# Dealing PSUM reads and gate steps over later units, accumulating DMAs in twos, and the last block's sums late from DRAM

## The chip, the cores and the metric

The kernel runs on one core of a Trainium2 chip. The metric is the device time of one execution in microseconds (us). A difference of some 0.3% (8 to 9 us here) is about what the measurement can tell from none.

## The reference, cut to what matters

```python
X = np.fft.fft(np.fft.fft(x, axis=1), axis=2).real          # x: 4 x 3072 x 256
h = X.reshape(12288, 256) @ w_in                             # 256 -> 2048
x = np.where(h > 0, h, np.exp(np.minimum(h, 0)) - 1) @ w_out # 2048 -> 256
h = np.maximum(x @ moe2_w_in, 0)                             # 256 -> 1024
u, v = h[..., :512], h[..., 512:]
v_n = (v - mean(v)) / np.sqrt(var(v) + 1e-6)                 # over the 512
v_s = einsum('ts,bsd->btd', w_spatial, v_n) + b_spatial      # 3072 x 3072, 4 batches
out = (u * v_s) @ moe2_w_out                                 # 512 -> 256
```

## The kernel before, in words

All matrix products are made in float32 as three products of rounded parts (`matmul3`, L180 to L182): a high part, which ScalarE (ACT) makes with a copy into the type fp32r, and a low part, the rest, which VectorE (DVE) makes with a subtraction. So every operand costs an ACT cast and a DVE subtraction before TensorE (PE) can use it.

The program has three stages. Up to about 170 us it makes the Fourier transform and prepares weights. From 170 to about 1290 us (the FFN stage) it works through 16 blocks of tokens, 8 groups to a block. While a block runs, the "pieces" of the block before it are made between its matmuls: six `v_piece` (one PSUM tile `pv`, ReLU on ACT at L670 into one of four buffers `v`, mean and deviation on GpSimd (POOL), the normalisation on DVE at L692) and eight `u_piece` (ACT at L717 into one of two buffers `uu`, then a DMA). The last stage does not use v itself but sums over subsets of its six token thirds: `V_SETS` lists 14 of them, and `v_d` holds one array of DRAM for each. A piece writes its v to the first array by a plain store on SyncE (SP, L735) and adds it to the others by accumulating DMAs on POOL's queue (L733), which `run_norms` issues all at once: up to five behind each other for one v. `finish` makes the pieces of the last block, while the last stage's first operands are prepared between them.

The last stage (from about 1300 us) is the product with w_spatial, by a scheme with 15 products instead of 18 (`PRODUCTS`). It is a list of 240 units (b, r, c, p): two batch pairs b, 15 products r, two column halves c, four steps p of the contraction. A unit is 24 matmuls 128x512 into the four PSUM banks `a` of its c. Its operand w is a sum of one to three blocks of w_spatial, its operand v one of the arrays above (a difference of two in one product); v is shared by the two c. Per unit the kernel writes down, in one fixed order on each engine, what I call emission k:

- if a gate is cut, `project` (24 matmuls 128x512 with w_out, names `gh`, `gl`, `wo2`) and `put` (ACT copy and store);
- `operands(k)`: `low` (DVE, L855, into `wlo` with two buffers or `vlo`) of the operands whose high part was made in emission k-1, that is those of unit k+1; `gate(k)`: one or two `multiply` (DVE, sum times u, L912) and, if a gate is being cut, four `cut_low` at once (DVE, L921, tile `gl`); `add` (DVE, L843, the sum of the loaded blocks `raw`, one instruction less than blocks) and `high` (ACT, L849) for unit k+2; and `load` (SP queue, L832, into one of 8 buffers `raw`) for unit k+4;
- the unit's 24 matmuls;
- after a unit with p = 3 its four `collect`, or eight where a product goes to two sums (DVE, L905: they read the PSUM banks into `sum`), all at once.

So DVE's order is the order of the emissions, and what is slow there delays the low parts behind it. Units 6 to 11 also load and convert w_out of the last product from a 64-bit format in four parts (`load_wo2`; names `wo2b`, `wo2r`, L146 to L166), each part using one `raw` buffer. The bounds of the emissions are not marked in the trace; the first unit starts at 1317.6 us, unit 16 at 1431.8, unit 239 at 2822.1.

Of the kernel before, what the change touches and what calls it, by code (L numbers as in the profile page):

```python
# [123 lines left out]
def fourier_ffn_gated_kernel(ctx: ExitStack, tc: tile.TileContext, t, out: bass.AP):  # L124
# [9 lines left out]
        for b in range(0, B, 2) for x in V_SETS for p in range(KP)  # L134
    }
    u_d = [[dram.tile([P, NJ, BLK], F32, name=f"u{b}{c}") for c in range(4)] for b in range(B)]

# [511 lines left out]
    def v_piece(i, k):  # L649
# [72 lines left out]
    def run_pieces(n):  # L722
        for _ in range(min(n, len(pieces))):
            kind, *a = pieces.pop(0)
            (v_piece if kind == "v" else u_piece)(*a)
        for d in deviations:
            d()
        deviations.clear()

    def run_norms(n=None):  # L730
# [15 lines left out]
    for s in range(NG + LAG):  # L746
# [76 lines left out]


    raws, highs, ready = {}, {}, {}

    def load(key):
        kind, k = key
        raws[key] = []
        for sg, src in (v_terms if kind == "v" else w_terms)(k):  # L830
            raw = rp.tile([P, 2, TC], F32, tag="raw", bufs=RAWS, name="raw")
            nc.sync.dma_start(raw, src)  # L832
            raws[key].append((sg, raw))

    def operand_tile(kind, x):
        if kind == "v":
            return th.tile([P, 2, HV], F32R, tag=f"v{x}", name=f"v{x}")
        return wq.tile([P, 2, TC], F32R, tag=f"w{x}", bufs=3 if x == "hi" else 2, name=f"w{x}")

    def add(*key):  # L840
        (_, x), *more = raws[key]
        for sg, y in more:
            nc.vector.tensor_tensor(x, x, y, op=ALU.add if sg > 0 else ALU.subtract)  # L843
        raws[key] = x

    def high(*key):
        x = raws.pop(key)
        hi = operand_tile(key[0], "hi")
        nc.scalar.copy(hi, x)  # L849
        highs[key] = hi, x  # L850

    def low(*key):
        hi, x = highs.pop(key)
        lo = operand_tile(key[0], "lo")
        nc.vector.tensor_tensor(lo, x, hi.bitcast(F32), op=ALU.subtract)  # L855
# [12 lines left out]

    us, biases, sums, parts, gates, gated, cutting = {}, {}, {}, {}, [], [], []

# [26 lines left out]
    def collect(b, r, c, accs, j, cols=slice(0, TC)):  # L897
# [8 lines left out]
        if j == NJ - 1:  # L906
            for n, m in completed(r):
                gates.extend(((b + n, MC * m + c), x) for x in range(NJ))

# [58 lines left out]

    def gate(k):


        for _ in range(2 if gates and gates[0][0][1] % MC == 1 or len(gates) > NJ or k >= NU - KP else 1):
            if gates:
                key, j = gates.pop(0)
                multiply(key, j)
                if j == NJ - 1:
                    gated.append((key, k))
                    del us[key]
        if cutting:
            for j in range(NJ):  # L980
                cut_low(cutting[0], j)

    def operands(k):

        for key in steps.get(k - 1, []) if k else []:
            low(*key)
        if gated and gated[0][1] < k and k + 1 < NU and idle(k + 1):
            key, _ = gated.pop(0)
            for j in range(NJ):
                cut_high(key, j)  # L990
            cutting.append(key)
        gate(k)
        for key in steps.get(k, []):
# [9 lines left out]
    for k in range(-2, 0):  # L1003
# [8 lines left out]
        finish(2)  # L1012
    finish(len(pieces) + 2)
    ffn.close()
    first.close()
# [8 lines left out]
    def bank(c, j):  # L1024
        return ps.tile([P, TC], F32, tag=f"a{c}{j}", name=f"a{c}{j}")

    accs = [None] * MC
    turn = 0
    for k, (b, r, c, p) in enumerate(units):
        if cutting:  # L1030
            key = cutting.pop()
            pos = [bank(1 - c, 2 * turn + o) for o in range(2)]
            turn = 1 - turn
            for j in range(NJ):
                project(key, pos, j)
            put(key, pos)
        operands(k)
        if WO2 <= k < WO2 + NJ:
            load_wo2(k - WO2)
# [22 lines left out]
        if p == KP - 1 and k < NU - 1:  # L1062
            for j in range(NJ):
                collect(b, r, c, accs[c], j)
    assert not gates and not gated and not cutting
    (n, m), = completed(r)
# [77 lines left out]
```

## Time and profile before

| | us |
|---|---|
| median of 3 runs | 2835.91 (2832.69 to 2841.42) |
| profiled execution | 2839.11, with a span of 2837.3 |
| PE busy | 2696.8 (95% of the span) |
| DVE busy | 2098.6 (74%) |
| ACT, POOL busy | 1308.7 (46%), 703.8 (25%) |
| mean granted TensorE clock | 0.977 |

The profiled execution took 3 us more than the median of the three runs. Its span leaves out 1.8 us around the program. All times of the trace count from the span's start. Busy matmuls are pipelined: one 128x512 matmul is shown as 0.39 us, but they start 0.227 us apart.

### The profile page before, as it was taken

The numbers are of one execution on the slowest core, as the hardware profiler recorded it, in microseconds if no ns is written. First come the engines' busy times: TensorE is split into PE (matmuls) and PEld (weight loads), VectorE is DVE, ScalarE is ACT, GpSimd is POOL, SyncE is SP. The second block draws the span as 40 slices with busy tenths as digits, with TensorE's granted clock in tenths as the row PEclk, the third lists the DMA queues.
The fourth block names the chain that finished last, engine by engine and source line by source line (L and its number), as shares of the span: only waits on it lengthen the run. The fifth ranks groups of instructions, "written<-read, shape, count | busy, mean of one in ns | idle before, by whom it ended". The sixth has DMA issues, their size and how long they took to land.

```text
span 2837.3 us, 35269 instructions
## 1 busy us (share of the span) xinstructions
PE 2696.8 (95%) x12854; PEld 2373.8 (84%) x12854; DVE 2098.6 (74%) x2541; ACT 1308.7 (46%) x1676; POOL 703.8 (25%) x1079
## 2 busy tenths in 40 slices
PE   5867999999999999997899999999999999999999
PEld 5757999999999999996687878787787887878877
DVE  8878888888878888883657657676756676676776
ACT  3456777777767777773222232333232222232332
POOL 5367244445543544456100000000000000000000
PEclk8989999999999999998899999999999999999999
DMA  5521466666774666779868668677767677677773
GB/s 224 184 74 42 154 144 144 142 152 144 145 150 152 144 154 148 147 164 260 262 224 283 226 215 274 230 261 251 252 207 262 228 244 251 227 259 249 260 242 135
DMA packets 211728, 561.15 MB, mean 198 GB/s; under 512 B 24777, under 2 KB 49370, under 8 KB 210018
## 3 DMA queue, kind: packets, MB, share of 16 engines
q1 hardware_dynamic: 145720, 435.10, 44.7%
q0 software_dynamic: 43520, 92.29, 18.0%
q10 hardware_dynamic: 22314, 31.51, 3.1%
q8 instruction: 100, 1.64, 0.2%
q14 instruction: 74, 0.61, 0.1%
HBM read 388.90 MB, written 169.91 MB: 197 GB/s over the span
## 4 chain that ended last, share of the span: by engine, by line
PE 72%; DVE 14%; DMA 4%; POOL 3%; issue 3%; ACT 3%; SPq 0%; ACTq 0%; DVEq 0%; POOLq 0%
PE a L181 13%; PE a L182 13%; PE a L180 13%; PE acc L181 5%; PE acc L182 5%; PE acc L180 5%; DVE raw L843 4%; DVE sum L905 2%; DVE vlo L855 2%; PE pv L181 1%; PE pv L180 1%; PE pv L182 1%; PE po L180 1%; PE pu L180 1%; PE po L181 1%
## 5 line engine op out<-in xcount | busy, mean ns | idle before, releaser
L181 PE MATMUL a<-wlo,vhi 128*128 128x512 f32 x1920 | 753.3, 392 | 18.0 <-DVE wlo L855 17.9
L182 PE MATMUL a<-whi,vlo 128*128 128x512 f32 x1920 | 752.8, 392 | 4.3 <-DVE vlo L855 4.3
L180 PE MATMUL a<-whi,vhi 128*128 128x512 f32 x1920 | 751.9, 392 | 1.6 <-ACT vhi L849 1.6
L849 ACT CAST whi<-raw 128x1024 fp32r<-128x1024 f32 x240 | 252.0, 1052 | 954.9 <-DVE raw L843 673.8
L855 DVE TENSOR_TENSOR wlo<-raw,whi 128x1024 fp32r<-128x1024 f32 x240 | 293.6, 1223 | 401.7 <-PE a L181 177.8
L181 PEld LDWEIGHTS a<-wlo,vhi 128*128 128x128 f32 x1920 | 362.8, 189 | 98.3 <-DVE wlo L855 22.1
L182 PEld LDWEIGHTS a<-whi,vlo 128*128 128x128 f32 x1920 | 363.1, 189 | 82.5 <-DVE vlo L855 6.6
L180 PEld LDWEIGHTS a<-whi,vhi 128*128 128x128 f32 x1920 | 363.2, 189 | 79.8 <-ACT vhi L849 3.4
L181 PE MATMUL acc<-glo,wo1h 128*128 128x384 f32 (+1 forms) x1024 | 350.9, 343 | 22.5 <-POOL glo L606 16.2
L180 PE MATMUL acc<-ghi,wo1h 128*128 128x384 f32 (+1 forms) x1024 | 348.6, 340 | 0.0
L182 PE MATMUL acc<-ghi,wo1l 128*128 128x384 f32 (+1 forms) x1024 | 348.2, 340 | 0.0
L894 POOL DMA_DIRECT2D u<-u x32 | 24.0, 752 | 1275.2 <-DVE sum L912 1000.5
L606 DVE TENSOR_TENSOR glo<-h,ghi 128x1536 fp32r<-128x1536 f32 (+3 forms) x128 | 221.0, 1727 | 137.7 <-ACT ghi L599 137.3
L843 DVE TENSOR_TENSOR raw<-raw 128x1024 f32<-128x1024 f32 x248 | 302.8, 1223 | 3.3
L733 POOL DMA_DIRECT2D v<-v x256 | 230.5, 1270 | 75.2 <-DVE v L692 46.4
L592 DVE SCALAR_TENSOR_TENSOR h<-e,h 128x1536 f32<-128x1536 f32 (+1 forms) x128 | 231.9, 1811 | 0.0
L581 ACT ACTIVATE e<-h 128x1536 f32<-128x1536 f32 (+1 forms) x128 | 190.0, 1484 | 88.6 <-DVE h L573 81.9
L181 PEld LDWEIGHTS acc<-glo,wo1h 128*128 128x128 f32 x1024 | 195.1, 191 | 28.8 <-POOL glo L606 18.8
L599 ACT CAST ghi<-h 128x1536 fp32r<-128x1536 f32 (+1 forms) x128 | 187.7, 1467 | 20.1 <-DVE h L592 20.1
L182 PEld LDWEIGHTS acc<-ghi,wo1l 128*128 128x128 f32 x1024 | 195.4, 191 | 0.0
L180 PEld LDWEIGHTS acc<-ghi,wo1h 128*128 128x128 f32 x1024 | 194.5, 190 | 0.1
L586 ACT ACTIVATE e<-e 128x1536 f32<-128x1536 f32 (+1 forms) x128 | 190.2, 1486 | 0.0
(198 smaller groups left out, 4441.9 us busy)
## 6 DMA issues: line engine op xcount, KB each, us to landing
raw<-in_wT SPq DMA_DIRECT2D x480, 512.0 KB, 5.2
v<-v POOLq DMA_DIRECT2D x256, 256.0 KB, 6.5
raw<-v SPq DMA_DIRECT2D x128, 512.0 KB, 4.1
v<-v SPq DMA_DIRECT2D x224, 256.0 KB, 3.0
u<-uu ACTq DMA_DIRECT2D x128, 192.0 KB, 3.5
u<-u POOLq DMA_DIRECT2D x16, 1024.0 KB, 7.5
q<-in_xq SPq DMA_DIRECT2D x12, 1032.0 KB
out<-sum SPq DMA_DIRECT2D x48, 256.0 KB, 2.1
```

What stands on the lines that cost most here:

```text
L180: nc.tensor.matmul(acc, lhsT=w[0], rhs=x[0], start=start, stop=False, skip_group_check=more)
L181: nc.tensor.matmul(acc, lhsT=w[0], rhs=x[1], start=False, stop=False, skip_group_check=more)
L182: nc.tensor.matmul(acc, lhsT=w[1], rhs=x[0], start=False, stop=stop, skip_group_check=more)
L581: nc.scalar.activation(e[:, :, :w], st[s]["h"][:, :, :w], AF.Relu, scale=-1.0)
L586: nc.scalar.activation(e[:, :, :w], e[:, :, :w], AF.Exp, scale=-1.0)
L592: nc.vector.scalar_tensor_tensor(out=h[:, :, :w], in0=e[:, :, :w], scalar=-1.0, in1=h[:, :, :w], op0=ALU.add, op1=ALU.max)
L599: nc.scalar.copy(st[s]["hi"][:, :, :w], st[s]["h"][:, :, :w])
L606: eng.tensor_tensor(st[s]["lo"][:, z, :w], st[s]["h"][:, z, :w], st[s]["hi"][:, z, :w].bitcast(F32), op=ALU.subtract)
L733: nc.gpsimd.dma_start(dst, v, accum_op=ALU.add)
L843: nc.vector.tensor_tensor(x, x, y, op=ALU.add if sg > 0 else ALU.subtract)
L849: nc.scalar.copy(hi, x)
L855: nc.vector.tensor_tensor(lo, x, hi.bitcast(F32), op=ALU.subtract)
```

## The change

Four things are done.

- In the last stage `operands(k)` keeps only `low`, `add`, `high` and `load`. What was in `gate`, and the `collect` at the end of a unit, goes into a queue (`waiting`, `keys`), and `rest(k, n)` behind `operands(k)` takes n pieces of it: `spare(k)` is 8, less two for each low part and each addition of the emission, eight more in the last 16 units and after a projection. Collects must go at the latest three units later. `project` comes once all four `cut_low` of a gate are written, in a unit whose other banks are free. One projection is left for after the last unit.
- `wlo` gets a third buffer. v is loaded straight into the buffer of its low part, `vlo`, where the subtraction then works in place; `raw` has 7 buffers for 8. The steps at which v is prepared move from (-6, -2, -1, 1) to (-6, -1, 0, 1).
- In the FFN stage the accumulating DMAs go into a list, and two are issued at a time (`run_sums(2)`), twice per group.
- The v of the last block is stored once, to a new array `v_last`, by plain stores on SP. Its 30 accumulating DMAs are issued in the last stage, from DRAM to DRAM, one every second unit from unit 16 on, on POOL's queue.

```diff
@@ norm (in v_piece)
+            if last:
+                stores.append((v_last[at // 2][:, at % 2], v, False))
+                return
@@ run_pieces, run_norms
+        run_sums(2)
+    def run_sums(n):
+        for dst, v in sums_due[:n]:
+            nc.gpsimd.dma_start(dst, v, accum_op=ALU.add)
+        del sums_due[:n]
             if more:
-                nc.gpsimd.dma_start(dst, v, accum_op=ALU.add)
+                sums_due.append((dst, v))
@@ the loop over the groups, behind run_norms()
+        run_sums(2)
@@ the last stage
-    RAWS = 8
+    RAWS = 7
+    HALVES = 8
+    LATE = 16
...
-        return p - 2 if r == 0 else MC * KP * r + (-6, -2, -1, 1)[p]
+        return p - 2 if r == 0 else MC * KP * r + (-6, -1, 0, 1)[p]
...
-    def gate(k):
-        for _ in range(2 if gates and gates[0][0][1] % MC == 1 or len(gates) > NJ or k >= NU - KP else 1):
-            if gates:
-                key, j = gates.pop(0)
-                multiply(key, j)
-                if j == NJ - 1:
-                    gated.append((key, k))
-                    del us[key]
-        if cutting:
-            for j in range(NJ):
-                cut_low(cutting[0], j)
+    def spare(k):
+        n = HALVES - 2 * len(steps.get(k - 1, []))
+        for kind, i in steps.get(k, []):
+            n -= 2 * (len((v_terms if kind == "v" else w_terms)(i)) - 1)
+        return n + (HALVES if k >= NU - 4 * KP else 0)
+
+    def rest(k, n):
+        while waiting and (n > 0 or waiting[0][0] <= k):
+            collect(*waiting.pop(0)[1:])
+            n -= 1
+        for x in keys:
+            while n > 0 and x["done"] < NJ:
+                multiply(x["key"], x["done"])
+                x["done"] += 1
+                n -= 1
...
+            while n > 0 and x["low"] < NJ and x["cut"] < k:
+                cut_low(x["key"], x["low"])
+                x["low"] += 1
+                n -= 1
@@ the loop over the units
-        if cutting:
-            key = cutting.pop()
+        n = spare(k)
+        if keys and keys[0]["low"] == NJ and idle(k) and not waiting:
+            key = keys.pop(0)["key"]
...
+            n += HALVES
         operands(k)
+        rest(k, n)
...
+        if LATE <= k and k % 2 == 0 and later:
+            dst, src = later.pop(0)
+            nc.gpsimd.dma_start(dst, src, accum_op=ALU.add)
...
         if p == KP - 1 and k < NU - 1:
-            for j in range(NJ):
-                collect(b, r, c, accs[c], j)
+            waiting += [(k + KP - 1, b, r, c, accs[c], j) for j in range(NJ)]
```

DVE of the kernel before, emissions 51 to 53 (a low part of v, the additions, the four reads of the banks after unit 51, and two gates cut right behind):

```order
L855 TENSOR_TENSOR vlo<-raw,vhi 128x1024
L843 TENSOR_TENSOR raw<-raw 128x1024 x2
L905 TENSOR_TENSOR sum<-bias,a_15020 128x512
L905 TENSOR_TENSOR sum<-bias,a_15021 128x512
L905 TENSOR_TENSOR sum<-bias,a_15022 128x512
L905 TENSOR_TENSOR sum<-bias,a_15023 128x512
L855 TENSOR_TENSOR wlo<-raw,whi 128x1024
L921 TENSOR_TENSOR gl<-sum,gh 128x512 x4
L843 TENSOR_TENSOR raw<-raw 128x1024 x2
L855 TENSOR_TENSOR wlo<-raw,whi 128x1024
L921 TENSOR_TENSOR gl<-sum,gh 128x512 x4
L843 TENSOR_TENSOR raw<-raw 128x1024 x2
```

The same gates in the kernel after: the first is multiplied and cut in emissions 44 to 47 (its projection stands ahead of unit 54, for 53 before):

```order
L932 TENSOR_TENSOR sum<-sum,u 128x512 x2
L876 TENSOR_TENSOR wlo<-raw,whi 128x1024
L932 TENSOR_TENSOR sum<-sum,u 128x512 x2
L876 TENSOR_TENSOR wlo<-raw,whi 128x1024
L860 TENSOR_TENSOR raw<-raw 128x1024 x2
L941 TENSOR_TENSOR gl<-sum,gh 128x512 x2
L876 TENSOR_TENSOR wlo<-raw,whi 128x1024
L860 TENSOR_TENSOR raw<-raw 128x1024 x2
L941 TENSOR_TENSOR gl<-sum,gh 128x512 x2
L876 TENSOR_TENSOR wlo<-raw,whi 128x1024
```

and the reads after unit 51 stand in emissions 52 and 53, in twos behind the additions, with the second gate's steps behind them (its projection is ahead of unit 57, for 54 before):

```order
L876 TENSOR_TENSOR wlo<-raw,whi 128x1024
L860 TENSOR_TENSOR raw<-raw 128x1024 x2
L926 TENSOR_TENSOR sum<-bias,a_14987 128x512
L926 TENSOR_TENSOR sum<-bias,a_14988 128x512
L876 TENSOR_TENSOR wlo<-raw,whi 128x1024
L860 TENSOR_TENSOR raw<-raw 128x1024 x2
L926 TENSOR_TENSOR sum<-bias,a_14989 128x512
L926 TENSOR_TENSOR sum<-bias,a_14990 128x512
L876 TENSOR_TENSOR wlo<-raw,whi 128x1024
L932 TENSOR_TENSOR sum<-sum,u 128x512 x4
L876 TENSOR_TENSOR wlo<-raw,whi 128x1024
L941 TENSOR_TENSOR gl<-sum,gh 128x512 x4
```

What moved: no low part of an operand stands behind four or eight reads and four cuts in a row any more.

POOL of the kernel before, in the last block's pieces (`v_...` are arrays of sums in DRAM, `v` the buffer in SBUF):

```order
L688 TENSOR_SCALAR w<-w 128x1
L689 TENSOR_TENSOR y<-y,w 128x1
L733 DMA v_1245_1_164<-v 128x512
L733 DMA v_245_1_172<-v 128x512
L733 DMA v_25_1_176<-v 128x512
L733 DMA v_35_1_184<-v 128x512
L733 DMA v_45_1_192<-v 128x512
L684 TENSOR_SCALAR ve<-sums 128x1
```

and POOL of the kernel after, behind the conversion of w_out in the last stage (`vl_...` is the new array):

```order
L166 TENSOR_TENSOR wo2r<-wo2r,wo2b_13783 128x256
L1082 DMA v_1245_1_164<-vl_195 128x512 x2
L1082 DMA v_1245_2_165<-vl_196 128x512 x2
L1082 DMA v_1245_3_166<-vl_197 128x512 x2
L1082 DMA v_245_1_172<-vl_195 128x512 x2
L1082 DMA v_245_2_173<-vl_196 128x512 x2
L1082 DMA v_245_3_174<-vl_197 128x512 x2
L1082 DMA v_25_1_176<-vl_195 128x512 x2
```

The 30 DMAs left the pieces of the last block, where six bursts of five stood; 14 of them stand ahead of the first `u` load of the last stage, with nothing of POOL's between them, 16 among the next such loads.

## Rows read from the trace of the kernel before

**Rows 1.** The page: busy time and share of the span, then DMA issues.

```profile
PE 2696.8 (95%) x12854; PEld 2373.8 (84%) x12854; DVE 2098.6 (74%) x2541; ACT 1308.7 (46%) x1676; POOL 703.8 (25%) x1079
...
raw<-in_wT SPq DMA_DIRECT2D x480, 512.0 KB, 5.2
```

**Rows 2.** What PE waited for, 1431.8 to 2822.1 us: total, times, longest.

```profile
PE a L181 <- DVE gl L921: 19.6, 8, 3.0
PE a L181 <- DVE wlo L855: 6.1, 5, 2.1
PE a L182 <- DVE vlo L855: 2.5, 4, 0.6
PE a L180 <- DVE sum L905: 1.2, 1, 1.2
```

**Rows 3.** Windows: length, then busy us (instructions) by engine, PEclk, DMA share, GB/s.

```profile
1291.50:1311.50 20.00, 11.70 (x42) 9.46 (x42) 6.44 (x11) 6.93 (x10) 14.54 (x28) 0.77 1.10 269
1317.60:1366.40 48.80, 46.61 (x194) 37.67 (x193) 22.23 (x23) 13.47 (x16) 19.37 (x28) 0.95 1.08 281
1366.40:1431.80 65.40, 52.40 (x194) 40.54 (x193) 44.60 (x59) 17.76 (x26) 7.75 (x7) 0.87 0.78 273
1431.80:1475.30 43.50, 43.50 (x193) 36.03 (x192) 21.51 (x22) 12.01 (x12) 0.00 (x0) 1.00 0.55 170
1475.30:1518.80 43.50, 43.50 (x193) 36.04 (x192) 29.48 (x29) 10.92 (x12) 0.00 (x0) 1.00 0.76 254
1518.80:1564.70 45.90, 43.88 (x193) 35.96 (x192) 38.02 (x41) 13.62 (x14) 0.00 (x0) 1.00 0.89 307
1636.00:1646.00 10.00, 6.70 (x23) 4.92 (x22) 8.48 (x12) 2.65 (x5) 0.00 (x0) 0.83 0.57 218
1858.40:1901.90 43.50, 43.50 (x194) 36.02 (x193) 36.72 (x38) 15.61 (x18) 0.75 (x1) 1.00 0.90 310
2044.00:2054.00 10.00, 7.90 (x35) 6.14 (x35) 8.77 (x12) 4.20 (x8) 0.00 (x0) 1.00 0.49 174
1431.80:2822.10 1390.30, 1360.51 (x5905) 1116.35 (x5904) 941.80 (x1018) 409.40 (x468) 21.66 (x29) 0.99 0.70 240
```

**Rows 4.** Timeline of DVE around 1636 us: start, us, work, idle ahead of it.

```profile
1636.30 2.48 DVE L905 TENSOR_TENSOR sum<-bias,a 128x512 f32<-128x512 f32 x4 [1.94 <-DMA bias<-in_moe_b_spatial]
1638.70 1.22 DVE L855 TENSOR_TENSOR wlo<-raw,whi 128x1024 fp32r<-128x1024 f32 x1
1639.83 2.49 DVE L921 TENSOR_TENSOR gl<-sum,gh 128x512 fp32r<-128x512 f32 x4
```

**Rows 5.** Timeline of PE at the same place.

```profile
1640.57 0.80 PE L181 MATMUL a<-gl,wo2h 128*128 128x512 f32 x1 [2.96 <-DVE gl L921]
```

**Rows 6.** Timeline of DVE around 1390 us.

```profile
1390.67 0.29 DVE L157 TENSOR_SCALAR wo2b<-wo2b 128x256 f32<-128x256 f32 x1 [1.63 <-ACT wo2b L155]
...
1392.00 1.22 DVE L855 TENSOR_TENSOR wlo<-raw,whi 128x1024 fp32r<-128x1024 f32 x1
```

**Rows 7.** Timeline of ACT around 1313 us.

```profile
1312.92 0.60 ACT L670 ACTIVATE v<-pv 128x512 f32<-128x512 f32 x1 [7.49 <-DMA v<-v]
...
1328.08 0.49 ACT L717 ACTIVATE uu<-pu 128x384 f32<-128x384 f32 x1 [5.94 <-DMA u<-uu]
```

**Rows 8.** Timeline of PE around 1313 us.

```profile
1313.57 0.69 PE L180 MATMUL pu<-x2hi,wi2h 128*128 128x384 f32 x1 [8.15 <-ACT v L670]
```

**Rows 9.** DMA queues and issues, 280 to 1250 us.

```profile
q0 software_dynamic: 29808, 54.28, 37.6%
...
v<-v SPq DMA_DIRECT2D x220, 256.0 KB, 3.0
v<-v POOLq DMA_DIRECT2D x207, 256.0 KB, 6.3
```

**Rows 10.** DMA queues and issues, 1300 to 1350 us.

```profile
q0 software_dynamic: 3481, 6.34, 70.7%
...
raw<-in_wT SPq DMA_DIRECT2D x8, 512.0 KB, 10.6
```

More of the change, by code (lines that the diff above doesn't have):

```diff
@@ L135, in fourier_ffn_gated_kernel @@
     }
+    v_last = {p: dram.tile([P, 2, HV], F32, name=f"vl{p}") for p in range(1, KP)}
     u_d = [[dram.tile([P, NJ, BLK], F32, name=f"u{b}{c}") for c in range(4)] for b in range(B)]
@@ L728, in run_pieces @@
         deviations.clear()
+        run_sums(2)
+    sums_due = []
+    def run_sums(n):
+        for dst, v in sums_due[:n]:
+            nc.gpsimd.dma_start(dst, v, accum_op=ALU.add)
+        del sums_due[:n]
     def run_norms(n=None):
@@ L867, in fourier_ffn_gated_kernel @@
         steps.setdefault(v_step(i), []).append(("v", i))
-    us, biases, sums, parts, gates, gated, cutting = {}, {}, {}, {}, [], [], []
+    us, biases, sums, parts, waiting, keys = {}, {}, {}, {}, [], []
     def reads(r):
@@ L906, in collect @@
         if j == NJ - 1:
-            for n, m in completed(r):
-                gates.extend(((b + n, MC * m + c), x) for x in range(NJ))
+            keys.extend({"key": (b + n, MC * m + c), "done": 0, "cut": None, "low": 0} for n, m in completed(r))
     def multiply(key, j, cols=slice(0, TC)):
@@ L967, in idle @@
         return p > 0 and not continued(r + (c == 1))
-    def gate(k):
-        for _ in range(2 if gates and gates[0][0][1] % MC == 1 or len(gates) > NJ or k >= NU - KP else 1):
-            if gates:
-                key, j = gates.pop(0)
-                multiply(key, j)
-                if j == NJ - 1:
-                    gated.append((key, k))
-                    del us[key]
-        if cutting:
-            for j in range(NJ):
-                cut_low(cutting[0], j)
+    def spare(k):
[12 more added lines that the diff above has]
+                n -= 1
+                if x["done"] == NJ:
+                    del us[x["key"]]
+        if keys and keys[0]["done"] == NJ:
+            x = keys[0]
+            if x["cut"] is None:
+                for j in range(NJ):
+                    cut_high(x["key"], j)
+                x["cut"] = k
+            while n > 0 and x["low"] < NJ and x["cut"] < k:
+                cut_low(x["key"], x["low"])
+                x["low"] += 1
+                n -= 1
     def operands(k):
@@ L986, in operands @@
             low(*key)
-        if gated and gated[0][1] < k and k + 1 < NU and idle(k + 1):
-            key, _ = gated.pop(0)
-            for j in range(NJ):
-                cut_high(key, j)
-            cutting.append(key)
-        gate(k)
         for key in steps.get(k, []):
@@ L1013, in fourier_ffn_gated_kernel @@
     finish(len(pieces) + 2)
+    run_sums(len(sums_due))
     ffn.close()
@@ L1025, in bank @@
         return ps.tile([P, TC], F32, tag=f"a{c}{j}", name=f"a{c}{j}")
+    later = [(v_d[B - 2, x, p][:, z], v_last[p][:, z]) for x in V_SETS if 5 in x for p in v_last for z in range(2)]
     accs = [None] * MC
@@ L1062, in fourier_ffn_gated_kernel @@
         if p == KP - 1 and k < NU - 1:
-            for j in range(NJ):
-                collect(b, r, c, accs[c], j)
-    assert not gates and not gated and not cutting
+            waiting += [(k + KP - 1, b, r, c, accs[c], j) for j in range(NJ)]
+    assert len(keys) < 2 and not waiting
+    for x in keys:
+        while x["low"] < NJ:
+            rest(NU + x["low"], NJ)
+        pos = [bank(1 - c, 2 * turn + o) for o in range(2)]
+        turn = 1 - turn
+        for j in range(NJ):
+            project(x["key"], pos, j)
+        put(x["key"], pos)
     (n, m), = completed(r)
```

36 lines of the change are left out of this document (21 added, 15 removed).

## The prediction

> **What bounds the kernel now.** The first view is the page: PE is busy for 95% of the span [rows 1], and the change takes no matmul away. So only the time in which PE waits, or works at its lower clock, can be had.
>
> The second is the windows [rows 3]. A stretch without a stall, such as 1431.8 to 1475.3, holds eight units, 192 matmuls, in 43.50 us: 0.2266 us a matmul, 5.44 us a unit. The reader is to hold every other stretch against this. From unit 16 to unit 239 (1431.8 to 2822.1) there are 223 units and 23 projections of 24 matmuls each, 5904 in all; at 0.2266 that is 1337.6 us, and it took 1390.3. **52.7 us are overhead**: 29.8 us in which PE was idle (1390.30 less 1360.51 busy), and 22.9 us in which its matmuls were longer than they need be.
>
> The third view says what the idle time waited for [rows 2]: `gl`, the low part of a gate, 19.6 us in eight waits; `wlo` 6.1, `vlo` 2.5, `sum` 1.2. All of it is DVE's. The timelines show how: at 1636.30 DVE reads the four banks after unit 51, then makes one `wlo`, then at 1639.83 the first cut [rows 4], and PE, whose projection needs it, has stood still for 2.96 us when it starts at 1640.57 [rows 5]. The reads can't begin before PE is done with the unit, so whatever DVE does between them and the cut is time that PE sees.
>
> The longer matmuls are the clock. In the ten us around that gap the granted clock is 0.83 [rows 3]: 0.17 of 10 us, taken twice since the low level is half of full speed, is 3.4 us at 1.2 GHz, or 1.7 us lost. The mean of 0.99 over the stage allows for 14 us of loss; the rest of the 22.9 I put down to PE's refilling behind a gap. The ten us from 2044 to 2054, with 2.1 us of idle time too, keep 1.00 [rows 3], so not every gap is punished. The Trainium skill ("TensorE: Matmul & The Clock Gate", section "HAM oscillation — how this bites in real kernels") says that waits between bursts of matmuls put the clock down again each time, at a cost of half of the time at the low level. [...]
>
> Two stretches ahead of unit 16 are worse. Eight units from 1366.4 to 1431.8 took 65.4 us for 43.5 [rows 3], 21.9 too many. Here w_out is converted: DVE waits 1.63 us for an ACT step on `wo2b` and only then comes to `wlo` at 1392.00 [rows 6]. And between the FFN stage and unit 0 PE was idle for 8.15 us in one piece, at 1313.57 [rows 8]: ACT's ReLU of a `v_piece` waited 7.49 us for a buffer `v` [rows 7], held by accumulating DMAs. The DMA share is above 1 there [rows 3], and POOL's queue has 70.7% of the engines [rows 10].
>
> **The change part by part.** *Reads and gate steps dealt out, third `wlo`.* The instructions stay the same in number and kind. DVE is busy for 941.8 of 1390.3 us [rows 3], 68%; in its heaviest stretch without projections for 38.02 us of what would be 43.5, 87%. So the work fits, and what matters is its order. Before, a low part for unit k+1 is written to the buffer that unit k-1 has just left; with three buffers it can be written from the start of unit k-1, two units or 10.9 us ahead of its use. Against this stands the longest emission of DVE. From the rows a low part or an addition takes 1.14 us of DVE's time in a row, a read or cut 0.61 (2.48 us for four). Most emissions of the new order then hold 2.3 to 4.8 us. The longest, with eight reads, hold 7.1 to 8.4, and one at unit 224 holds 11.9 but with 2.4 us left when counted from the end of the unit that it reads. None reaches what the buffer gives. Four cuts now end a unit or more ahead of their projection, so the `gl` waits go, and the `wlo`, `vlo` and `sum` waits with them: 29.8 us. Without gaps there is no clock loss and no refilling: up to 22.9 us more. I take 44 of the 52.7, since some first wait or clock dip will be left; bounds 20 (the `gl` waits alone) and 52.7.
>
> *`vlo` in place, 7 `raw`, other steps for v.* No work is added; a low part of v comes an emission later at most. A load of v waits on SP until unit k-1 has left `vlo`, and the loads of w queue behind it; they are issued two emissions, 10.9 us, ahead and land in 5.2 [rows 1]. Cost: nothing. The cover ends where the landing passes 10.9 us.
>
> *The last block's sums.* Six bursts of five accumulating DMAs leave the way between the stages; six plain stores take their place, which land in 3.0 us [rows 9] (they wait for their normalisation on SP, with loads for units 0 to 2 behind them; those had waited for the engines, so I charge nothing, at most one landing of 3.0). So the 7.49 us wait of ACT goes and with it PE's 8.15 us. The waits of the `uu` buffers stay (5.94 us at 1328.08 [rows 7]), though the engines are freer. I take 9 us at unit 0 and 2 more at unit 2, where the loads landed in 10.6 us [rows 10]: 11, bounds 4 and 16 (all idle time of these pieces and some clock, 0.77 over 20 us [rows 3], which is 4.6 us).
>
> *Conversion of w_out.* ACT and DVE still hand `wo2b` to each other in the emission of the low parts, so I don't take all of the 21.9. But the low parts have one more unit of room, and the loads are no longer behind the accumulating DMAs. I take 9; bounds 0 and 18.
>
> *Twos in the FFN stage.* The same DMAs in another rhythm; PE waits little there. I take 1, bounds -3 and 3.
>
> *The 30 DMAs from DRAM.* In the FFN stage POOL's queue had 37.6% of 970 us for 207 of them: 1.76 us of all engines each [rows 9]. 30 are 53 us. From unit 16 on the engines were busy for 0.70 of 1390 us [rows 3], so 417 us are free; hidden. But POOL waits for nothing before it issues them: 14 stand behind each other, and the `u` loads among the next eight have free buffers, so about 22 go in one burst behind the conversion, in the two or three products where the share is 0.55, 0.76 and 0.89. 22 are 39 us of engine time; free there are 19.6, 10.4 and 4.8 us, 34.8, and the rest is taken up by the loads' lead. No row has such a DMA from DRAM to DRAM. Its cost is bounded below by a plain load (310 GB/s at a share of 0.90 [rows 3] make 0.76 us for 256 KB) and above by a landing that has all engines to itself, 6.3 us [rows 9]. I take 1.76, since the destination is read and written in the same way and only the source differs. Behind the burst on POOL's queue stand `u` loads alone; the first gate is not multiplied before emission 44, some 150 us on.
>
> Sum: 44 + 11 + 9 + 1 = 65 us. On the profiled execution's 2839.1 that gives 2774, a span of 2772; the median of the runs shown is 3 us under that execution: 2771. I say **2772**.
>
> **The rivals.** *Slower: the burst starves the loads.* Place: units 14 to 50. What speaks for it: with 70.7% of the engines on POOL's queue, loads of `raw` landed in 10.6 us for 5.2 [rows 1, 10]. If POOL's queue takes half while it has work, 22 DMAs of c us each last 44c us, and the loads get 0.5. At 1.76 that is 77 us: the loads fall behind by 0.05 of 43.5 us and 0.26 of 34, 11 us, just their lead. For a larger c they want about 0.73 (the mean of the three shares), so they fall behind by 10c, and what passes the lead of 11 us is PE's delay: at c = 3.5 some 24 us, a total of 2798; at 6.3, 52 us and 2826. The whole gain of 65 is gone at c = 7.6, four times the row; at 9 the time is 2774 + 79 = 2853. Against it: the 207 rows. The Trainium skill ("DMA: Bandwidth & Descriptors", section "Queues, rings and completion order") says that each engine goes round between the queues with work, packet by packet. By this rule the burst would indeed be served beside the loads and not after them; rows 10 agree in direction.
>
> *Half the gain.* The gaps of the w_out conversion and the transition stay, and each product with three blocks keeps a gap that halves the clock: 20 + 4 + 0 + some clock, about 30: 2806. For it: DVE has 87% in the heaviest stretch, so a late start there is made up slowly. Against it: the buffer's 10.9 us.
>
> *The stalls are the loads', not DVE's.* Most stalls of the steady part lie where products have three blocks and the DMA share is 0.89. Then dealing out DVE's work gains nothing there, and only 11 + 9 are left: 2816. Against it: 1858.4 to 1901.9 has 0.90 and 310 GB/s and runs in 43.50 us without a stall [rows 3]; what differs is DVE's 36.7 us, without a cut.
>
> *Nothing changes*, if gains early are given back by the burst: 2830 to 2840.
>
> **How the numbers follow.** Forecast (2750 to 2795) 0.68; half the gain 0.14; loads 0.06; nothing 0.05; slower 0.07. 0.3% is 8.5 us, about what a measurement tells from no change. Faster: 0.68 + 0.14 + 0.06 = 0.88, less 0.01 for a half that ends near 2828: 0.87; same 0.06; slower 0.07. The range leaves out 0.05 below 2750 (all bounds at their best: 2839 - 90) and, above 2814, the last three cases with most of the loads' case, 0.15. The likeliest case's own range is 2750 to 2795.
>
> **What would show it right or wrong.** Right: no wait of PE on `gl` and hardly one on `wlo` from unit 16 on; eight units in 43.5 us also in the products with three blocks; granted clock 1.00 there; unit 0 near 1308 and unit 16 some 20 us earlier than 1431.8; ACT's `v` waiting for no DMA. Wrong: PE waiting on `wlo`, with DVE waiting in turn for `raw` between units 14 and 50 (the burst), a 65 us stretch still at the conversion, new waits of the FFN stage on `v` at the fifth v of a block, or a wait on `gl` that has moved to the projections' new places.

## The result, and the profile after

The kernel after took 2788.54 us (median of 4 runs, 2786.33 to 2790.58), the kernel before 2837.6 in the same comparison (4 runs): a ratio of 0.983, with an interval of 0.981 to 0.985. It is faster by 49 us. 2772 were forecast, a gain of 65, with a range of 2750 to 2814.

Where did the 49 us come from? The page first: busy time and share by engine. PE's busy share is up by one point only [rows 1], so the gain must be looked for by stage.

```profile
PE 2679.0 (96%) x12854; PEld 2363.4 (85%) x12854; DVE 2107.6 (76%) x2541; ACT 1311.1 (47%) x1676; POOL 711.2 (26%) x1079
```

The windows of the kernel after, cut where the work changes: blocks 1 to 15 of the FFN stage (first matmul of `acc` of each), then up to unit 0, to unit 2, to unit 16, to unit 239, to the end. Columns as in [rows 3].

```profile
276.00:1235.80 959.80, 950.96 (x5210) 920.99 (x5209) 806.25 (x1038) 682.44 (x854) 448.44 (x809) 1.00 0.63 147
1235.80:1327.20 91.40, 79.67 (x403) 74.37 (x402) 52.83 (x71) 49.45 (x69) 47.01 (x92) 0.93 0.72 173
1327.20:1338.10 10.90, 10.90 (x49) 9.02 (x49) 7.09 (x9) 4.50 (x5) 2.85 (x9) 1.00 0.72 234
1338.10:1426.80 88.70, 82.19 (x338) 65.70 (x338) 60.16 (x72) 24.55 (x32) 19.58 (x20) 0.94 0.81 256
1426.80:1470.30 43.50, 43.50 (x193) 36.03 (x192) 21.66 (x22) 12.53 (x12) 7.34 (x9) 1.00 1.07 326
1470.30:1513.80 43.50, 43.50 (x193) 36.04 (x192) 32.53 (x32) 12.22 (x12) 0.00 (x0) 1.00 0.90 331
1426.80:2764.00 1337.20, 1335.19 (x5881) 1103.50 (x5880) 938.39 (x1016) 408.27 (x463) 35.95 (x46) 1.00 0.74 256
2764.00:2787.70 23.70, 17.57 (x79) 13.54 (x77) 10.54 (x19) 7.50 (x15) 0.00 (x0) 0.96 0.18 67
```

The first four of these stretches in the kernel before (its last two are 1390.30 us [rows 3] and the 15.2 us from 2822.1 to the end):

```profile
274.90:1224.20 949.30, 945.53 (x5211) 920.51 (x5210) 796.31 (x1038) 681.06 (x854) 440.74 (x809) 1.00 0.64 148
1224.20:1317.60 93.40, 80.12 (x404) 74.87 (x403) 53.45 (x71) 48.10 (x66) 56.87 (x103) 0.92 0.84 195
1317.60:1331.00 13.40, 11.85 (x49) 9.38 (x47) 2.92 (x5) 3.99 (x7) 11.71 (x20) 0.94 1.06 245
1331.00:1431.80 100.80, 87.15 (x337) 68.83 (x338) 63.91 (x78) 27.24 (x35) 15.40 (x16) 0.90 0.89 281
```

The reader subtracts the lengths line by line:

| stretch | before | after | gained | forecast |
|---|---|---|---|---|
| up to block 1 | 274.9 | 276.0 | -1.1 | 0 |
| FFN stage, blocks 1 to 15 | 949.3 | 959.8 | **-10.5** | +1 |
| block 15 to unit 0, unit 2 | 93.4 + 13.4 | 91.4 + 10.9 | **+4.5** | +11 |
| unit 2 to 16 (conversion of w_out) | 100.8 | 88.7 | +12.1 | +9 |
| unit 16 to 239 | 1390.3 | 1337.2, with one projection (5.4) less | **+47.7** | +44 |
| behind unit 239 | 15.2 | 23.7, with that projection | -3.1 | 0 |

The sum is 49.6, which is the difference of the spans, 2837.3 less 2787.7. The steady part did what was expected and a little more. In the list of what PE waited for there, where [rows 2] had four lines and 29.4 us (a fifth, 0.3 us for ACT's `gh`, is not shown there), there is one line:

```profile
PE a L182 <- DVE gl L941: 2.0, 1, 2.0
```

The late DMAs are a burst as foreseen, and hidden as foreseen: from 1426.8 to 1470.3 the DMA share is 1.07 and the eight units still take 43.50 us at a clock of 1.00. But the FFN stage, which was charged with next to nothing, became 10.5 us longer. Its waits (line waited for, total, times, longest):

```profile
PE pe L181 <- DVE q L567: 5.1, 7, 1.4
PE po L181 <- ACT uu L721: 2.7, 4, 1.9
PE acc L182 <- DVE glo L607: 1.1, 5, 0.3
```

`q` is made by DVE, whose seven late ones are a new line. The timelines of the first of them, in block 3, say why (start, length, work, idle time ahead). POOL of the kernel after:

```profile
430.73 0.92 POOL L739 DMA_DIRECT2D v<-v  x1 [0.26 <-PE po L183]
431.40 2.16 POOL L148 TENSOR_TENSOR xlo<-xraw,xhi 128x772 fp32r<-128x772 f32 x1
```

DVE of the kernel after at the same time:

```profile
431.34 3.85 DVE L607 TENSOR_TENSOR glo<-h,ghi 128x1536 fp32r<-128x1536 f32 x1 [1.02 <-ACT ghi L600]
435.11 0.60 DVE L567 SCALAR_TENSOR_TENSOR q<-xmid,wmid,pe 128x384 f32<-128x384 f32 x1
```

and PE of the kernel after:

```profile
435.76 0.44 PE L181 MATMUL pe<-xhi,weh 128*128 128x384 f32 x1 [0.75 <-DVE q L567]
```

An accumulating DMA of the twos is issued at 430.73; behind it on POOL stands the low part of the next block's x (`xlo`), which so starts at 431.40, 0.06 us behind DVE's `glo`. Both subtract float32 tiles in SBUF. `glo` takes 3.85 us for its usual 1.76; the 2.1 us more are about the length of `xlo`. `q` then comes late, and PE stands for 0.75 us. In the kernel before the same pair passed each other: there POOL had no DMA at this place and `xlo` had run from 428.16 to 430.03, and `glo` from 429.70. POOL of the kernel before:

```profile
428.16 1.87 POOL L147 TENSOR_TENSOR xlo<-xraw,xhi 128x772 fp32r<-128x772 f32 x1
```

DVE of the kernel before:

```profile
429.70 1.94 DVE L606 TENSOR_TENSOR glo<-h,ghi 128x1536 fp32r<-128x1536 f32 x1 [2.81 <-ACT ghi L599]
```

The Trainium skill ("SBUF — State Buffer", section "Who interferes with whom") says this outright: a DVE instruction with both inputs in SBUF contends with a GpSimd instruction that reads SBUF. The trace agrees: 1.94 us where they overlap by 0.33, 3.85 where all of `xlo` lies inside `glo`.

The 10.5 us are in two halves. PE was idle for 8.8 us of the stage (959.80 less 950.96 busy), against 3.8 before. The other 5.4 us are in busy time: behind a stop the first matmul is shown 0.44 us long for 0.34, as at 435.76, and behind a stop of 1.9 us for `uu` at 828 the clock stood at its half level for 3.4 us. Window of the kernel after, with the granted clock of 0.83 over ten us:

```profile
826.00:836.00 10.00, 8.15 (x38) 7.83 (x38) 5.13 (x6) 5.55 (x6) 5.87 (x11) 0.83 0.54 111
```

In the eight kernels with twos (this one and e2 to e7 and e12 below) the longest such wait for `uu` is 1.9 to 2.6 us, and the clock fell there in five of them; in the six without (the kernel before, e1, e8 to e11) it is 1.3 to 1.6 us and the clock stayed at 1.00. So the twos lengthen this wait as well; by what way was not tried.

### The profile page after: what moved, and what is told of

Its sections match the earlier page's. It is cut to its first block, busy times and chain, and to the rows that moved or that the text cites. A ratio compares the mean times of both kernels' runs of the same rounds, so it can differ in the third digit from the quotient of the medians.

```text
span 2787.7 us, 35149 instructions
## 1 busy us (share of the span) xinstructions
PE 2679.0 (96%) x12854; PEld 2363.4 (85%) x12854; DVE 2107.6 (76%) x2541; ACT 1311.1 (47%) x1676; POOL 711.2 (26%) x1079
## 4 chain that ended last, share of the span: by engine, by line
PE 79%; DVE 9%; ACT 5%; DMA 3%; POOL 3%; issue 1%; ACTq 0%; SPq 0%; DVEq 0%; POOLq 0%
PE a L182 17%; PE a L183 16%; PE a L181 16%; PE acc L182 5%; PE acc L183 5%; PE acc L181 5%; DVE glo L607 2%; PE pv L183 1%; DMA u<-uu 1%; PE pv L181 1%; PE pv L182 1%; PE pe L181 1%; ACT ghi L600 1%; PE po L181 1%; PE po L182 1%
## 5 line engine op out<-in xcount | busy, mean ns | idle before, releaser
L182 PEld LDWEIGHTS a<-wlo,vhi 128*128 128x128 f32 x1920 | 361.3, 188 | 81.5 <-DVE wlo L876 6.0
L607 DVE TENSOR_TENSOR glo<-h,ghi 128x1536 fp32r<-128x1536 f32 (+3 forms) x128 | 231.2, 1806 | 139.3 <-ACT ghi L600 139.3
L860 DVE TENSOR_TENSOR raw<-raw 128x1024 f32<-128x1024 f32 x240 | 293.0, 1221 | 11.0 <-DMA raw<-in_wT 7.8
L739 POOL DMA_DIRECT2D v<-v x226 | 204.7, 1259 | 52.9 <-DVE v L693 38.4
```

Source lines behind the costliest of these rows:

```text
L182: nc.tensor.matmul(acc, lhsT=w[0], rhs=x[1], start=False, stop=False, skip_group_check=more)
L607: eng.tensor_tensor(st[s]["lo"][:, z, :w], st[s]["h"][:, z, :w], st[s]["hi"][:, z, :w].bitcast(F32), op=ALU.subtract)
L860: nc.vector.tensor_tensor(res, total, y, op=ALU.add if sg > 0 else ALU.subtract)
```

## The experiments

All times of stretches are from the profiled execution of each kernel; where a time of the whole is given without a range, it is that one execution's. How far they repeat is seen on what is alike in several kernels: the FFN stage as in the kernel after took 957.2 to 959.8 us in the six kernels that have it (after, e4 to e7, e12), the stretch from block 15 to unit 0 91.4 to 92.2 in five of them.

**The FFN stage.** *e1: the sums at once again.*

```diff
             if more:
-                sums_due.append((dst, v))
+                nc.gpsimd.dma_start(dst, v, accum_op=ALU.add)
```

> The FFN stage's accumulating DMAs are issued at once again, up to five in a row, as in the kernel before; everything else is as in the kernel after. From the first acc matmul of block 1 to that of block 15 the kernel before took 949.3 us, the kernel after 959.8. Theory (POOL's order): the twos stand ahead of the x split on POOL, so POOL's xlo subtraction runs at the same time as DVE's glo subtraction and stretches it to 3 to 4.5 us for 1.75; PE then waits for q. Expected: 949 to 951 us, glo never above 2.7 us, execution 2778 to 2781. Rival (the length comes from what else changed, such as buffers and arrays): 958 to 961, execution about 2789.

*e2: the second two of a group behind the x split.*

```diff
         deviations.clear()
-        run_sums(2)
...
                 split_x(groups[s][0] + 1)
+        if step >= 0:
+            run_sums(2)
... finish, for the last block's pieces
                 run_pieces(2)
+                run_sums(2)
```

> The DMAs stay in twos, but the second two of a group are issued at the end of the group, behind the x split, in place of ahead of it. Theory (POOL's order): xlo starts some 1.2 us earlier, overlaps glo less; blocks 1 to 15 take 949 to 955 us, glo above 3 us at most once or twice. Rival (the rhythm of the twos loads the DMA engines or POOL in another way, wherever they stand): 957 to 961.

*e3: xlo on DVE.*

```diff
-        split(hi[:, :, :n], lo[:, :, :n], raw[:, :, :n], nc.gpsimd if i else None)
+        split(hi[:, :, :n], lo[:, :, :n], raw[:, :, :n], None)
```

> The kernel after, with the low part of x (xlo, once per block) made on DVE and not on POOL; DMAs in twos as they are. Theory (the two engines stretch each other when both read float32 from SBUF): DVE gets about 0.9 us more per block, but no glo is above 2.7 us; blocks 1 to 15 take 949 to 954 us. Rival (PE's waits come from DVE being late for another reason): 958 to 963, with glo still above 3 us in places.

Measured for blocks 1 to 15: e1 950.0 us (execution 2775.0, 3 us under the range expected, since the stretch behind it is shorter too), e2 950.6 (2780.5), e3 955.6 (2787.3). The view that decides is the group of `glo` on DVE: duration in ns, minimum, median and maximum. The kernel after:

```profile
L607 DVE TENSOR_TENSOR glo<-h,ghi x112: 958/1759/4466, 279.3 to 1228.7; 128x1536 fp32r<-128x1536 f32 x86, 128x1540 fp32r<-128x1540 f32 x24, 128x768 fp32r<-128x768 f32 x2
```

The same group of e1:

```profile
L607 DVE TENSOR_TENSOR glo<-h,ghi x113: 958/1760/2583, 279.3 to 1229.4; 128x1536 fp32r<-128x1536 f32 x87, 128x1540 fp32r<-128x1540 f32 x24, 128x768 fp32r<-128x768 f32 x2
```

The same group of e2:

```profile
L607 DVE TENSOR_TENSOR glo<-h,ghi x113: 958/1759/2612, 279.9 to 1231.3; 128x1536 fp32r<-128x1536 f32 x87, 128x1540 fp32r<-128x1540 f32 x24, 128x768 fp32r<-128x768 f32 x2
```

The same group of e3:

```profile
L607 DVE TENSOR_TENSOR glo<-h,ghi x112: 959/1759/1766, 280.2 to 1225.8; 128x1536 fp32r<-128x1536 f32 x86, 128x1540 fp32r<-128x1540 f32 x24, 128x768 fp32r<-128x768 f32 x2
```

e2 keeps the twos and moves only where they stand against `xlo`, and wins back 9 of 10.5 us: it is POOL's order. e3 keeps the order and takes POOL's read away, and the longest `glo` is 1.77 us: the lengthening of `glo` is the two engines reading at once. As a cure e3 is poor, and its range was missed by 1.6 us: `q` is gone from PE's waits, but only 4.2 of the 10.5 us came back, since PE's busy time is 951.98 us, against 945.53 in the kernel before. Two things in its trace bear on that: a clock fall as in the kernel after (3.4 us at half level, behind a wait of 2.2 us for `uu`), and a new line of DVE's waits, which must now stand for ACT's `xhi` before it can make `xlo`:

```profile
DVE xlo L148 <- ACT xhi L147: 32.1, 14, 4.2
```

What each of them costs was not tried.

**Between the stages.** *e5: the last two pieces of block 14 late as well.*

```diff
-    v_last = {p: ... for p in range(1, KP)}
+    v_last = {p: ... for p in range(KP)}
...
-            if last:
+            if b == B - 1 and e == 5:
                 stores.append((v_last[at // 2][:, at % 2], v, False))
```

> The kernel after, with the last two v pieces of block 14 treated as those of block 15: stored once, their 10 accumulating DMAs among the late ones. From the first acc matmul of block 15 to unit 0 the kernel before took 93.4 us, the kernel after 91.4, with ACT's v waiting 7.58 us for a DMA of v. Theory: that wait is for these ten DMAs; without them 80 to 86 us, execution 2780 to 2784. Rival (the DMA engines are full with the first loads of the last stage, and the uu buffers hold PE as well): 88 to 92 us.

*e8: the last block's sums back between the stages.*

```diff
-            if last:
-                stores.append((v_last[at // 2][:, at % 2], v, False))
-                return
...
-    later = [(v_d[B - 2, x, p][:, z], v_last[p][:, z]) for ...]
+    later = []
```

> As e1_sums_at_once, with the 30 accumulating DMAs of the last block back where they were before the change, in bursts of five out of the buffers v; no late DMA. In e1 block 15 to unit 0 took 87.0 us, unit 0 to 16 99.3, the execution 2775.0. Theory (the late DMAs free the way between the stages and cost little later): block 15 to unit 0 92 to 95 us, unit 0 to 16 99 to 106, execution 2781 to 2789. Rival (what they give early they take back as a burst at units 12 to 16): sum of both stretches within 3 us of e1's 186.3, execution 2772 to 2778.

*e9: v through raw.*

```diff
-            if kind == "v" and not raws[key]:
-                raw = th.tile([P, 2, HV], F32R, tag="vlo", name="vlo")
-                nc.sync.dma_start(raw.bitcast(F32), src)
-            else:
-                raw = rp.tile([P, 2, TC], F32, tag="raw", bufs=RAWS, name="raw")
-                nc.sync.dma_start(raw, src)
+            raw = rp.tile([P, 2, TC], F32, tag="raw", bufs=RAWS, name="raw")
+            nc.sync.dma_start(raw, src)
...
-        lo = x if key[0] == "v" else wq.tile(...)
+        lo = th.tile(..., tag="vlo", ...) if key[0] == "v" else wq.tile(...)
```

> As e8_last_block_back (sums at once, last block's sums back between the stages), with v loaded into raw and its low part written to vlo by a subtraction that doesn't work in place, as before the change; 7 raw as after. From block 15 to unit 0 e8 took 101.6 us, the kernel before 93.4, with the same accumulating DMAs in both. Theory (loading v into vlo, which comes free later, moves the first loads of the last stage together with the accumulating DMAs): 92 to 96 us. Rival (the third wlo and the seventh raw make it): 100 to 103 us. Unit 16 to 239: 1337 to 1345 us by both, longer if 7 raw are too few for w and v together.

| us | block 15 to unit 0 | unit 0 to 16 | execution |
|---|---|---|---|
| before | 93.4 | 114.2 | 2839.1 |
| e9: sums at once, none late, v by raw | 93.5 | 120.1 | 2800.4 |
| e8: the same, v into vlo | 101.6 | 103.1 | 2791.6 |
| e1: e8 with the last block's 30 late | 87.0 | 99.3 | 2775.0 |
| after: e1 with twos | 91.4 | 99.6 | 2789.5 |
| e5: after with 10 more late | 81.5 | 97.3 | 2776.9 |

The table is read downwards. Loading v into `vlo` costs 8 us here (e9 to e8) and gives 17 back in the next stretch, where w, v and w_out would share seven `raw`. Taking the 30 DMAs out gives 14.6 (e8 to e1), the twos take 4.4 of it (e1 to after), and ten more late DMAs give 9.9 (after to e5). e5 and e9 lie in the ranges of their theories for the stretch (e5's execution is 3 us under its own). e8 lies in neither: 101.6 us for 92 to 95, an execution of 2791.6 for 2781 to 2789, and the two stretches together 18 us above e1's; neither theory nor rival knew of the cost of `vlo`. Where the wait sits is seen on ACT. Its timeline in the kernel after:

```profile
1304.35 0.49 ACT L721 ACTIVATE uu<-pu 128x384 f32<-128x384 f32 x1 [6.67 <-DMA u<-uu]
...
1320.16 0.60 ACT L671 ACTIVATE v<-pv 128x512 f32<-128x512 f32 x1 [7.58 <-DMA v<-v]
```

The 7.58 us are what [rows 7] had as 7.49: a `v_piece` waits for a buffer whose sums are still under way. They are now those of block 14's last two pieces, since block 15 has none any more. The 6.67 us ahead of it are the wait for `uu` that was expected to stay. In e5 ACT waits for no DMA of `v` between the stages; the `uu` line, which stayed in all kernels, is on top of its waits:

```profile
ACT uu L721 <- DMA u<-uu: 11.5, 4, 5.1
```

That the way of v costs 8 us is shown by e9; what probably stands behind it is seen on SP. The first load of v is issued at 1281.05 us in e8, at 1266.92 in e9 and at 1266.38 in the kernel before, so in e8 it shares the engines with accumulating DMAs. That this alone makes the 8 us is argued and was not tried. SP of e8:

```profile
1281.05 0.32 SPq L846 DMA_DIRECT2D vlo<-v  x1
```

SP of the kernel before:

```profile
1266.38 0.93 SPq L832 DMA_DIRECT2D raw<-v  x1
```

**The late burst.** *e4: the late DMAs from unit 50 on.*

```diff
-    LATE = 16
+    LATE = 50
```

> The kernel after with its 30 late DMAs written down from unit 50 on, not 16, so that they stand behind the first u loads on POOL's queue, which wait for buffers. In the kernel after 22 of them go in one burst from 1400 us on, DVE waits 2.1 and 1.4 us for blocks of w at 1413, and unit 0 to unit 16 takes 99.6 us (87.0 without a stall). Theory (the burst costs PE the stalls of units 13 and 15): 94 to 97 us. Rival (those stalls are the conversion of w_out's): 98 to 100 us. Both expect 1337 to 1340 us from unit 16 to unit 239.

98.2 us for unit 0 to 16, against 99.6, and e7, whose late DMAs are those of the kernel after, has 97.8: the rival's range. Only five late DMAs are then issued at that place, on POOL of e4:

```profile
1401.20 4.28 POOL L1082 DMA_DIRECT2D v<-vl  x5
```

and DVE of e4 waits for the same blocks of w all the same:

```profile
1412.71 1.22 DVE L860 TENSOR_TENSOR raw<-raw 128x1024 f32<-128x1024 f32 x1 [2.47 <-DMA raw<-in_wT]
1415.31 1.22 DVE L860 TENSOR_TENSOR raw<-raw 128x1024 f32<-128x1024 f32 x1 [1.37 <-DMA raw<-in_wT]
```

Five late DMAs are still there, but e8 has none at all, and DVE waits at the same place:

```profile
1418.89 2.59 DVE L857 TENSOR_TENSOR raw<-raw 128x1024 f32<-128x1024 f32 x2 [2.10 <-DMA raw<-in_wT]
```

So the burst does not make these stalls; my theory fell. That the conversion makes them is what is left, and SP of e8 speaks for it (1380 to 1425 us): its loads of w wait for `raw` buffers which w_out holds until `wo2r` is made. No run left the conversion out.

```profile
SPq L849 <- DVE wo2r L167: 5.9, 4, 2.3
```

The burst is not free without end, though: with 40 late DMAs e5 shows gaps of 0.63 and 0.63 us at unit 18, and its unit 16 to 239 takes 1339.1 us for 1337.2.

How fast the late DMAs go depends on what runs beside them. In e4 each issue waits for the landing of an earlier one; from 1655.65 to 1663.71 us, where POOL's queue has a share of 1.04 of the engines and the loads' queue 0.08, one lands every 1.2 to 1.6 us. POOL of e4:

```profile
1656.89 0.81 POOL L1082 DMA_DIRECT2D v<-vl  x1 [0.42 <-DMA v<-vl]
1658.12 0.81 POOL L1082 DMA_DIRECT2D v<-vl  x1 [0.42 <-DMA v<-vl]
```

In the burst of the kernel after, where from 1400 to 1450 us the two queues have 0.53 and 0.50, one lands every 2.2 to 3.0 us up to 1440:

```profile
1413.91 0.81 POOL L1082 DMA_DIRECT2D v<-vl  x1 [1.75 <-DMA v<-vl]
1416.55 0.81 POOL L1082 DMA_DIRECT2D v<-vl  x1 [1.82 <-DMA v<-vl]
```

**The steady part.** *e6: two wlo; e7: no small portions; e12: both.*

```diff
e6, e12
-... tag="wlo", bufs=3
+... tag="wlo", bufs=2
e7, e12
-    HALVES = 8
+    HALVES = 100
```

> The kernel after with two buffers for wlo, as before the change; reads and gate steps stay dealt out. Unit 16 to 239 took 1390.3 us before (23 projections) and 1337.2 after (22). Theory (the room of a third buffer is what takes the waits): 1350 to 1375 us, with waits on wlo in the products with three blocks. Rival (dealing out alone does it): 1337 to 1341.

> The kernel after with room for 100 pieces in each emission, not 8: all reads of a unit stand in the next emission, the four multiplies with them, the four cuts at once in the next; still behind the low parts and additions, still with three wlo. The longest emissions of DVE grow from 7 to 8.4 us to 8.4 to 9.5, two reach 11.9. Theory (third buffer and place behind the low parts do it, not the small portions): 1338 to 1345 us from unit 16 to 239. Rival (the small portions do it): over 1350, with gl waits of 2 to 3 us at most projections.

> The kernel after with both e6's and e7's edit: two wlo, and room for 100 pieces in each emission. What stays of the dealing is the place: low parts and additions first, reads behind them, a projection only when its four cuts are written. e6 took 14.2 us more than the kernel after from unit 16 to 239, e7 10.4. Without any gain the stretch would take 1384.9 us (1390.3 less the one projection that moved behind the last unit). Theory (the place does most of it): 1355 to 1370 us, about the sum of the two. Rival (room and small portions stand in for each other, and without both the gain is gone): 1375 to 1390.

Unit 16 to 239: after 1337.2, e6 1351.4, e7 1347.6, e12 **1404.6** us. For e6 the theory's range held, but without the waits on `wlo` that it named: 6.1 of its 14.2 us are at one place, between the units 225 and 226 (19.3 us for 13.2). e7 lies between its two; 6.5 of its 10.4 us are at one place too, between the units 105 and 106. e12 is above both of its ranges, and decides: with neither the third buffer nor the small portions the stretch is 19.7 us longer than the 1384.9 of the kernel before, and the waits of [rows 2] are back and larger. (Why it is longer than before, and not the same, was not tried: it still has the other places of the reads, `vlo` in place and seven `raw`.) What PE waited for in e12:

```profile
PE a L182 <- DVE gl L941: 22.6, 5, 5.8
PE a L181 <- DVE sum L926: 14.0, 5, 3.0
PE a L182 <- DVE wlo L876: 3.4, 2, 1.9
```

So the two stand in for each other: either takes 33 to 37 us of the 47.7, and without both nothing is left. What one emission's work looks like when it isn't dealt out, in e7 at unit 106 (DVE): eight reads and four multiplies, and only behind the next low parts and additions the cut at 1957.13 for which PE waited 3.62 us.

```profile
1945.40 4.87 DVE L926 TENSOR_TENSOR sum<-sum,a 128x512 f32<-128x512 f32 x8
1950.18 2.50 DVE L932 TENSOR_TENSOR sum<-sum,u 128x512 f32<-128x512 f32 x4
1952.59 1.22 DVE L876 TENSOR_TENSOR wlo<-raw,whi 128x1024 fp32r<-128x1024 f32 x1
1953.73 1.22 DVE L876 TENSOR_TENSOR vlo<-raw,vhi 128x1024 fp32r<-128x1024 f32 x1
1954.86 1.22 DVE L860 TENSOR_TENSOR raw<-raw 128x1024 f32<-128x1024 f32 x1
1956.00 1.22 DVE L860 TENSOR_TENSOR raw<-vlo,raw 128x1024 f32<-128x1024 f32 x1
1957.13 2.50 DVE L941 TENSOR_TENSOR gl<-sum,gh 128x512 fp32r<-128x512 f32 x4
```

**A better version.** *e10: e1 and e5, and the copies of the left-over projection behind the last one's steps; e11: the eight more pieces one unit later.*

```diff
e10, e11 (beside the edits of e1 and e5)
-        put(x["key"], pos)
+        left = [(x["key"], pos)]
...
             project(key, pos, *at)
+    for x in left:
+        put(*x)
     put(key, pos)
e11
-        return n + (HALVES if k >= NU - 4 * KP else 0)
+        return n + (HALVES if k > NU - 4 * KP else 0)
```

> The kernel after with sums at once (e1), the late DMAs of block 14's last two pieces (e5), and the copies of the left-over projection (put) written down behind the last projection's steps, so that ACT comes to the last casts earlier. Theory (the gains of e1 and e5 are apart from each other): blocks 1 to 15 950 us, block 15 to unit 0 80 to 83 us, the stretch behind unit 239 at most 22.5 us for 23.7; 2765 to 2770 us, ratio to the kernel before 0.975 to 0.978. Rival (both gains are the same wait of ACT's v, and the put frees nothing): 2772 to 2777.

> As e10_best, with the eight more pieces of the last units from unit 225 on, not 224, so that the eight reads after unit 223 are not waited for in the emission right behind it. Theory (the gl wait of 2.0 us at unit 226 comes from that emission of 11.9 us, and takes 2 us of clock with it): that wait goes, unit 16 to 239 in 1333 to 1335 us for 1337.2, the execution 3 to 4 us under e10_best. Rival (the wait moves to the projection of unit 227): 1337 us and no difference.

e10 took 2762.71 us (4 runs, 2760.70 to 2765.43), a ratio to the kernel before of 0.973, interval 0.9715 to 0.9745: below the range expected. Blocks 1 to 15 took 949.5 us. Its windows up to unit 0 and behind unit 239 (20.6 us for 23.7):

```profile
1225.00:1304.60 79.60, 75.25 (x404) 71.08 (x404) 51.30 (x70) 49.01 (x68) 36.68 (x80) 1.00 0.62 156
2743.00:2763.60 20.60, 16.68 (x79) 13.77 (x77) 10.53 (x19) 7.52 (x15) 0.00 (x0) 1.00 0.21 77
```

e11 took 2763.74 (0.9735, 0.9718 to 0.9752): the two can't be told apart, though in the trace the wait at the projection of unit 226 (2.01 us) became one of 0.77 at 227 and the stretch from unit 16 on 2.7 us shorter (1338.0 for 1340.7). The 1333 to 1335 us and the gain of 3 to 4 us that were expected did not come.

## Why the prediction was right, and where it was off

The direction and the mechanism of the largest term were right, and the time lay in the range; the point was 16 us too low. That it was not further off is partly luck: the FFN stage, the pieces of the last block and the end came out 21 us worse than forecast, the conversion and the steady part 7 us better. Two of the signs set up for being right were not seen: unit 0 came at 1327.2 us and not near 1308, and ACT's `v` still waits for a DMA. By its steps:

- *Reads and gate steps dealt out, third `wlo`* (+44): right, 47.7. The condition, that DVE's longest emission stays within what the buffer gives, is what e12 broke, though PE's waits there are on `gl` and `sum` and for 3.4 us only on `wlo`. The text credited the buffer with the room and the dealing with the `gl` waits; in truth either does most of both. The emission at unit 224, given 2.4 us to spare, has none: it leaves the one wait of 2.0 us. On the clock the text was near: from unit 16 on the trace of the kernel before has 30.7 us at half level, 15.4 us lost, where it allowed for 14. But 12 of its 19 gaps were followed by no fall, not only the one that the text names.
- *Twos in the FFN stage* (+1, bounds -3 and 3): this step failed. It priced the DMAs' rhythm and left out what is queued behind them on POOL: `xlo`, pushed by about a microsecond into `glo`. The stage became 10.5 us longer; e1 (back to 950.0) shows that it is the twos, e2 (950.6) that it is their place ahead of `xlo`, e3 that `glo` is lengthened by POOL's `xlo` and nothing else. The trace of the kernel before would have told: `glo` there takes 1.92 to 2.58 us wherever it meets `xlo`, for 1.76.
- *The last block's sums* (+11, bounds 4 and 16): 4.5. Taking the sums away is worth more than was said, 18.4 us by e1 against e8 (14.6 between the stages, 3.8 behind). But ACT's wait did not go, as the step had it: it moved to the sums of block 14's last pieces, 7.58 us in the kernel after and still 5.0 in e1; e5, which takes these away too, has none. And two other parts of the change took from it, which were charged with nothing: `vlo` 8 us by e9 and e8, the twos 4.4. In the text "cost: nothing" for `vlo` was argued from the steady part; at the start v is loaded later by this way.
- *Conversion of w_out* (+9): 12.1, by chance nearer than its working: `vlo` beside seven `raw` makes 17 us there (e9 to e8). Of the two reasons given, the room of the third `wlo` is worth 4.2 us of it (unit 2 to 16 in 92.9 us in e6, 88.7 in the kernel after), and the accumulating DMAs out of the way 0.7 (89.1 in e8, 88.4 in e1).
- *The 30 DMAs from DRAM*: hidden, as said. Each took about 1.45 us of all engines, below the 1.76 taken (an estimate from e4, 1655.65 to 1663.71 us: 828 packets in a share of 1.036, at the 144 packets to a DMA that [rows 9] give). The rival was right that POOL's queue takes half of the engines while it has work (0.53), so that one goes every 2.6 us or so; but PE was not delayed by 30 of them, and by 40 only at unit 18 (1.8 us, e5).
- Not priced: the projection left for the end, whose copies stand on ACT ahead of the last casts, 3.1 us; e10 took them back.

## What to carry to other kernels

When instructions are moved on a queue, list what stands behind them there and which engine works at the time to which it is pushed: a DMA issue of 0.9 us on POOL, ahead of `xlo`, went with up to 2 us more for a block (69.5 us for 67.4 in block 3). Room in time (another buffer) and small portions of work can each cure the same stall; try each alone and neither, or their worth is put down to the wrong one. A wait for a buffer that is held by slow DMAs can move to the next holder when the first is served, as here (7.49 us before, 7.58 after): look who holds it then.

## What the runs showed of the hardware

A float32 subtraction on DVE (`glo`) and one on POOL (`xlo`), both from SBUF, lengthened each other. In the kernel after `glo` took 1.95 us for 1.76 where the two overlapped by 0.33, 2.57 at 0.95, 2.98 at 1.35, 3.85 at 2.16 and 4.47 at 2.50; `xlo`, 1.87 us by itself, took 2.16 and 2.50 in the last two. In one of the fourteen pairs it was the other way: `glo` had begun 0.85 us earlier and kept its length, and `xlo` took 2.64. DVE and POOL of the kernel after:

```profile
636.94 1.76 DVE L607 TENSOR_TENSOR glo<-h,ghi 128x1536 fp32r<-128x1536 f32 x1 [0.67 <-ACT ghi L600]
637.79 2.64 POOL L148 TENSOR_TENSOR xlo<-xraw,xhi 128x768 fp32r<-128x768 f32 x1
```

With `xlo` on DVE no `glo` was above 1.77 us (e3). Accumulating DMAs of 256 KB from DRAM to DRAM went one every 1.2 to 1.6 us where nearly nothing ran beside them (e4) and one every 2.2 to 3.0 us beside the loads of w (kernel after). A DMA share of 1.07 for 43.5 us did not delay PE at all where loads were issued two emissions ahead.
